# Attention and two MLPs on one core: the first MLP product is taken as (softmax)(state w_in), and part of its squares goes to GpSimd

## Chip, cores and metric

One core of a Trainium2 chip runs the whole program in one launch. The metric is the device time of one execution in microseconds (us), median of several runs; less is better.

## What is computed

```
scores = 0.125 * x @ state^T ; a = softmax(scores) ; xread = a @ state        # per (b, h)
scores2 = 0.125 * state @ x^T ; a2 = softmax(scores2) ; sread = a2 @ x
X = concat([xread, sread]) -> tokens x (h d)                                   # 2176 x 512
h = X @ w_in ; g = where(h >= 1, h, where(h <= -1, 0, (h + 1)^2 / 4)) ; Y = g @ w_out    # 512 -> 2048 -> 512
out = ((Y @ w_a) * (Y @ w_b)) @ w_out2                                         # 512 -> 1536 -> 512
```

There are 4 batches b of 8 heads h, 512 tokens and 32 state rows for each, head width d = 64. Activations come as float32, the weights as 8-byte floats that are turned into float32 on the chip. The tolerance asks for nearly float32 products.

## The kernel before, in words

**Order.** The program records every operation with its engine, its inputs and outputs as byte ranges and PSUM banks, and a rough cost (class `Flow`). `Flow.order` then lays out all engines' instructions: the matmul operations keep the order in which they were recorded, except those marked `loose` (the attention ones), and everything else is placed by due time. All DMAs are issued from one queue, SyncE's (SP), in that order. Each engine works its instructions off strictly in order, with semaphores between engines.

**Products.** A float32 operand is split into a high part (`hi_of`, a ScalarE copy to float32r) and a low part (`tt`, a VectorE subtraction); a product is then three matmuls (`three`, hi*hi, hi*lo, lo*hi), recorded by `mms` (L333 of the profile). Weights are converted by `conv` (L357: the load; L377 or L309: two byte casts on VectorE/ScalarE; L383: a shift-and-or on VectorE).

**Stage one (`phase_one`).** For each of 8 pairs k (half a batch, 4 heads) attention computes scores (`a_qk`, L488), the softmax over 32 state rows (`a_soft`, L504 to L522: transpose, maximum, a subtraction on GpSimd, exp on ScalarE, sum, a multiplication on GpSimd, transpose) and xread (`a_read`, L544 or L536), which is split into the x tiles. `s_soft`, `s_tr` (L596) and `s_read` (L610) make sread. Then `h_mm(j, f)` makes 128 columns f of h for a block j of tokens: 5 blocks of 512, 512, 512, 320 and 320 tokens, 16 values of f, contraction 512 in 4 tiles, so 12 matmuls into one of four PSUM banks. Behind each of these 80 units stand `relu` on ScalarE (L658), `square` on ScalarE, a min/max on VectorE that reads the bank again (L665), and the store of g to DRAM (L300). In this stage the weights w_out (for stage two) are converted too, and part of the second MLP's weights are converted and stored to DRAM as `u_d`.

**Stages two and three.** `v_all` makes the seven operands of a Strassen-like scheme out of w_out, and `b_chunk` runs g @ w_out in three chunks of tokens, each from g loaded back from DRAM, 7 products of 48 matmuls (128 x 368) per chunk. Then `ab_run` and `o_run` do the second MLP. These are L333 matmuls as well.

Of the kernel before, what the change touches and what calls it, by code (L numbers as in the profile page):

```python
# [9 lines left out]
F32 = mybir.dt.float32  # L10
# [9 lines left out]
class Flow:  # L20
# [141 lines left out]
def attention_then_two_mlps(  # L162
# [13 lines left out]
    nc = tc.nc  # L176
# [16 lines left out]
    UA = 4  # L193
    ONDVE = 0
    HALVES = 2
    STEPS = (0, 2, 8, 12, 17, 21, 25, 29)
# [31 lines left out]
    class V2:  # L228
# [97 lines left out]
    def mms(b, cols, pairs, first, last, n, rd, onto=False, off=0):  # L326
# [10 lines left out]
        op({"PE": n * t_mm(cols)}, emit, rd, [bank(b)])  # L337
# [59 lines left out]
    arenas["R0"] = pc.tile([P, R0 // 4], F32R, name="r0")  # L397
# [5 lines left out]
    u_d = pd.tile([F2 + 4, P, 512], F32, name="u_d")  # L403
# [4 lines left out]
    w32_a = Ring([V("F1", 4096 * i, 1024) for i in range(2)])  # L408
# [4 lines left out]
    win = {f: [V("R0", 512 + 8192 * (f // 2) + 2048 * (f % 2) + 4096 * h, 512) for h in range(2)] for f in range(F1)}  # L413
    XAT = [512 + 65536, 512 + 81920, 512 + 114688, 512 + 65536, 512 + 98304]
    x = [[V("R0", XAT[j] + 4 * 4 * BLK[j] * i, 4 * BLK[j]) for i in range(2)] for j in range(NB)]

    def w_in(f, k):
        d, r = conv(w1_k[0, f : f + k], k, stage_a(), z_a(), by="DVE")
        hi, lo = (V("R0", win[f][h].at, 512 * k) for h in range(2))
        hi_of(hi, lambda: d(F32), 512 * k, r, regs(hi))  # L420
        tt(lo, lambda: d(F32), lambda: hi(F32), ALU.subtract, 512 * k, r + regs(hi), regs(lo))

    def aset(arena, o):
        names = (("xld", 1024), ("xn", 1024), ("st", 256), ("t1", 512), ("at", 512), ("a2t", 512))
# [23 lines left out]
    def x_parts(t0, n):  # L448
        done = 0
        while done < n:  # L450
            j = max(i for i in range(NB) if OFF[i] <= t0 + done)
            m = min(n - done, OFF[j] + BLK[j] - t0 - done)
            yield j, t0 + done - OFF[j], done, m
            done += m
# [8 lines left out]
    def a_qk(k):  # L463
# [3 lines left out]
        if "w3" in d:  # L467
            split(*d["s3"], d["st"].sub(128, 128))
        if "x3" in d:
            for i in range(2):  # L470
                split(*(v.sub(512 * i, 512) for v in d["x3"]), d["xld"].sub(512 * i, 512))
            split(*d["q3"], d["st"].sub(0, 128))

            def emit3(e):
                for k, (w, x) in enumerate(three(d["q3"], d["x3"])):
                    for p in range(2):
                        r = slice(64 * p, 64 * p + 64)
                        nc.tensor.matmul(
                            banks[b][r, :], w()[:, r], x()[:, p * 512 : (p + 1) * 512], start=k == 0, stop=k == 2
                        )  # L480

            op({"PE": 0.72}, emit3, regs(*d["q3"], *d["x3"]), [bank(b)], loose=True)
            return
# [8 lines left out]
        op({"PE": 1.8}, emit, regs(d["st"], d["xld"]), [bank(b)], loose=True)  # L492
# [7 lines left out]
    def a_soft(k):  # L500
# [6 lines left out]
            {"DVE": 0.69} if k < ONDVE else {"POOL": 1.35},  # L507
# [793 lines left out]
```

## Time and profile before

| | |
|---|---|
| three runs | 796.75, 798.03, 798.40 us; median 798.03 |
| profiled execution, first to last instruction | 793.9 us |
| TensorE matmul busy | 779.2 us (98%) |
| VectorE busy | 565.4 us (71%) |
| ScalarE busy | 462.5 us (58%) |
| GpSimd busy | 18.8 us (2%) |
| moved by DMA | 130.05 MB, 164 GB/s over the span |

The profiled execution has no run time of its own in the record: its span is 793.9 us, 4.1 us under the median of the runs, which also hold what lies before the first and behind the last instruction. Busy shares are means over stages with different limits, so the prediction reads the first stage by itself.

### The profile page before, as it was taken

The numbers are of one execution on the slowest core, as the hardware profiler recorded it, in microseconds if no ns is written. First come the engines' busy times: TensorE is split into PE (matmuls) and PEld (weight loads), VectorE is DVE, ScalarE is ACT, GpSimd is POOL, SyncE is SP. The second block draws the span as 40 slices with busy tenths as digits, with TensorE's granted clock in tenths as the row PEclk, the third lists the DMA queues.
The fourth block names the chain that finished last, engine by engine and source line by source line (L and its number), as shares of the span: only waits on it lengthen the run. The fifth ranks groups of instructions, "written<-read, shape, count | busy, mean of one in ns | idle before, by whom it ended". The sixth has DMA issues, their size and how long they took to land.

```text
span 793.9 us, 12498 instructions
## 1 busy us (share of the span) xinstructions
PE 779.2 (98%) x4814; PEld 736.8 (93%) x4814; DVE 565.4 (71%) x810; ACT 462.5 (58%) x714; POOL 18.8 (2%) x22
## 2 busy tenths in 40 slices
PE   5999999999999999999999999999999999999998
PEld 3676788879999999999999999999999999999997
DVE  6899863645377885886999897656463679987661
ACT  3889995877676444445665676655422455544440
POOL 2101210000000000000000000000000000000000
PEclk7999999999999999999999999999999999999999
DMA  6879783787226581270433466746151137554211
GB/s 245 295 238 318 246 272 107 247 282 261 91 93 190 165 264 39 79 215 28 130 132 111 131 216 218 242 133 207 55 195 49 37 111 261 170 169 128 99 42 40
DMA packets 76859, 130.05 MB, mean 164 GB/s; under 512 B 6016, under 2 KB 52608, under 8 KB 76800
## 3 DMA queue, kind: packets, MB, share of 16 engines
q1 hardware_dynamic: 76800, 129.26, 49.7%
q8 instruction: 37, 0.61, 0.3%
q14 instruction: 22, 0.18, 0.1%
HBM read 84.93 MB, written 44.30 MB: 163 GB/s over the span
## 4 chain that ended last, share of the span: by engine, by line
PE 87%; DMA 4%; DVE 4%; ACT 3%; issue 1%; SPq 0%; POOL 0%; ACTq 0%; DVEq 0%; POOLq 0%
PE bank L333 84%; DMA f<-in_w_dram 4%; ACT f L309 2%; DVE f L383 1%; PE bank L610 1%; DVE r L318 1%; ACT r L309 1%; DMA f<-in_st_dram 1%; PE bank L488 1%; PE bank L536 0%; DVE f L665 0%; PE bank L596 0%; SPq L297 0%; DVE f L505 0%; DVE f L377 0%
## 5 line engine op out<-in xcount | busy, mean ns | idle before, releaser
L333 PE MATMUL bank<-r 128*128 128x368 f32 (+4 forms) x3048 | 527.7, 330 | 2.7 <-DVE r L318 0.8
L333 PEld LDWEIGHTS bank<-r 128*128 128x128 f32 x3048 | 484.9, 189 | 33.7 <-issue 5.4
L318 DVE TENSOR_TENSOR r<-f,r 128x736 fp32r<-128x736 f32 (+7 forms) x225 | 221.4, 993 | 65.8 <-ACT r L309 62.1
L309 ACT ACTIVATE r<-f 128x736 fp32r<-128x736 f32 (+7 forms) x225 | 193.8, 871 | 123.1 <-PE bank L333 99.4
L333 PE MATMUL bank<-r,r 128*128 128x368 f32 (+2 forms) x1512 | 238.9, 313 | 0.7 <-DVE f L318 0.7
L333 PEld LDWEIGHTS bank<-r,r 128*128 128x128 f32 x1512 | 229.1, 189 | 1.0 <-DVE f L318 1.0
L309 ACT ACTIVATE f<-bank 128x368 f32<-128x368 f32 (+3 forms) x191 | 87.3, 460 | 145.3 <-PE bank L333 144.9
L309 ACT ACTIVATE f<-f 128x512 f32<-128x512 f32 (+5 forms) x157 | 131.5, 854 | 22.3 <-POOL f L508 8.9
L318 DVE TENSOR_TENSOR f<-bank,f 128x368 f32<-128x368 f32 (+2 forms) x168 | 85.3, 517 | 77.0 <-PE bank L333 68.4
L318 DVE TENSOR_TENSOR f<-f 128x256 f32<-128x256 f32 (+6 forms) x146 | 120.0, 843 | 2.1 <-DMA f<-p_d 1.0
L665 DVE SCALAR_TENSOR_TENSOR f<-f,bank 128x512 f32<-128x512 f32 (+1 forms) x80 | 47.4, 602 | 41.2 <-ACT f L309 35.2
L658 ACT ACTIVATE f<-bank,half 128x512 f32<-128x512 f32 (+1 forms) x80 | 49.4, 617 | 29.3 <-PE bank L333 25.2
L383 DVE SCALAR_TENSOR_TENSOR f<-f 128x1024 uint32<-128x1024 uint32 (+1 forms) x39 | 43.7, 1120 | 18.7 <-ACT f L309 18.6
L318 DVE TENSOR_TENSOR f<-f,f 128x736 f32<-128x736 f32 (+1 forms) x24 | 21.6, 909 | 1.0 <-DMA f<-g_d 0.9
L318 DVE TENSOR_TENSOR r<-bank,r 64x64 fp32r<-64x64 f32 (+3 forms) x36 | 14.5, 418 | 7.6 <-ACT r L309 7.4
L610 PEld LDWEIGHTS bank<-f 128*128 128x128 f32 x128 | 15.3, 192 | 1.4 <-ACT f L309 0.9
L610 PE MATMUL bank<-f 128*128 128x64 f32 x128 | 15.3, 273 | 0.1
L309 ACT ACTIVATE r<-bank 64x64 fp32r<-64x64 f32 (+3 forms) x36 | 12.8, 376 | 4.2 <-PE bank L544 1.7
L544 PE MATMUL bank<-f 64*128 64x512 f32 x16 | 5.5, 766 | 5.0 <-DVE f L522 4.9
L488 PE MATMUL bank<-f 128*64 128x512 f32 x32 | 8.6, 617 | 1.2 <-DMA f<-in_st_dram 1.2
L504 DVE STREAM_TRANSPOSE f<-bank 128x512 f32<-128x512 f32 x8 | 5.7, 711 | 5.0 <-PE bank L488 4.9
L544 PEld LDWEIGHTS bank<-f 64*128 64x128 f32 x16 | 1.4, 216 | 7.0 <-DVE f L522 6.3
(33 smaller groups left out, 94.8 us busy)
## 6 DMA issues: line engine op xcount, KB each, us to landing
f<-in_w_dram SPq DMA_DIRECT2D x29, 1024.0 KB, 6.0
f<-p_d SPq DMA_DIRECT2D x17, 768.0 KB, 4.9
g_d<-f SPq DMA_DIRECT2D x48, 256.0 KB, 5.3
f<-g_d SPq DMA_DIRECT2D x32, 368.0 KB, 4.0
p_d<-f SPq DMA_DIRECT2D x48, 184.0 KB, 2.0
f<-g_d SPq DMA_DIRECT2D x16, 352.0 KB, 3.7
f<-in_w_dram SPq DMA_DIRECT2D x10, 512.0 KB, 4.0
g_d<-f SPq DMA_DIRECT2D x32, 160.0 KB, 1.8
```

The costliest lines, as they stand in the source:

```text
L309: lambda e: nc.scalar.activation(dst(), src(), func, **{k: (v() if callable(v) else v) for k, v in kws.items()}),
L318: op({"DVE": t_tt(n)}, lambda e: nc.vector.tensor_tensor(dst(), a(), b(), alu), rd, wr)
L333: nc.tensor.matmul(o, w, x, start=first and k == 0, stop=last and k == n - 1, skip_group_check=onto)
L383: lambda e: nc.vector.scalar_tensor_tensor(out(U32), words_of(1, U32)(), 5, z(U32), ALU.logical_shift_right, ALU.bitwise_or),
L488: nc.tensor.matmul(banks[b][r, :], d["st"]()[:, r], d["xld"]()[:, p * 512 : (p + 1) * 512], start=True, stop=True)
L504: op({"DVE": 0.72}, lambda e: nc.vector.transpose(t1(), banks[b]), [bank(b)], regs(t1))
L544: nc.tensor.matmul(banks[ab], d["st"]()[r, 128:], d["at"]()[r, :], start=True, stop=True)
L610: nc.tensor.matmul(banks[ab][:, p * 64 : (p + 1) * 64], d["xn"]()[:, c * 256 + p * 128 : c * 256 + (p + 1) * 128], d["a2t"]()[:, c * 128 + ...
L658: lambda e: nc.scalar.activation(q(), h(), AF.Relu, bias=half[:, 0:1], scale=0.5),
L665: lambda e: nc.vector.scalar_tensor_tensor(g(), q(), 1.0, h(), ALU.min, ALU.max),
```

## The change

In stage one, xread is no longer formed. For each batch the 256 state rows (8 heads of 32) are multiplied with w_in first: `w_state(b, q, n)` makes, in plain float32 matmuls, 128 of these rows against 512 columns, and splits the result. `h_mm` then takes the softmax weights themselves (8 heads x 32 = 256) as contraction: 2 tiles instead of 4, so 6 matmuls per unit. There are now 4 blocks of 512 tokens; the 128 sread tokens go through `h_state`, plain float32 matmuls without a split. w_in itself is no longer split, nor are x tiles.

```diff
-    def h_mm(j, f, cs=range(4)):
+    def w_state(b, q, n):
+        d = qs[2 * b + q]
+        ab = abank()
+        def emit(e):
+            for p in range(2):
+                r = slice(64 * p, 64 * p + 64)
+                c = (2 * q + p) * P
+                w = win()[:, 2048 * n : 2048 * (n + 1)].rearrange("p (f x) -> p f x", x=512)[:, :, c : c + P]
+                nc.tensor.matmul(
+                    banks[ab][r, :].rearrange("p (f x) -> p f x", x=P), d["st"]()[:, r], w, start=True, stop=True
+                )
+        op({"PE": 1.05}, emit, regs(d["st"], win.sub(2048 * n, 2048)), [bank(ab)])
+        hi, lo = wsum[n][q]
...
+    def h_mm(j, f, cs=range(2)):
...
+            for q in cs:
+                out += three([v()[:, P * o : P * o + P] for v in wsum[n][q]], [v() for v in att[2 * j + q]])
...
+        def square(e):
+            if e == "ACT":
+                nc.scalar.activation(g(), g(), AF.Square)
+            else:
+                nc.gpsimd.tensor_tensor(g(), g(), g(), ALU.mult)
+        op({"ACT": t_act(512), "POOL": 1.1}, square, regs(g), regs(g))
...
+    def h_state(n):
...
+            for i in range(4):
+                w = win.sub(2048 * n + 512 * i, 512)()
+                for c in range(4):
+                    nc.tensor.matmul(
+                        banks[b][:, P * i : P * i + P],
+                        w[:, P * c : P * c + P],
+                        xs()[:, P * c : P * c + P],
...
-    UA = 4
+    UA = 0
+    SWITCH = 48
+    FETCH = (-14, -9, -4, -1)
...
+        if self.gate is not None and size:
+            deps.add(self.gate)
```

The square of each unit is placed by `Flow.order` on ScalarE or on GpSimd (46 of 68 land on GpSimd, L622 of the changed kernel). The memory plan is new: an arena `FS` holds w_in, the attention tiles and four of the seven output buffers, and is given up after unit 48 for `RH` and `F1`, which take the operands of stage two. `flow.gate` keeps some loads (those of w_out, and of the first chunk's g) from being issued before a given unit. The operands of w_out are split in three steps (`v_early`, `v_upper`, `v_rest`). `UA = 0` and the new `w_sums` move eight half-megabyte weight conversions of the second MLP out of stage one: four into the third chunk of stage two, four into stage three.

Names in the rows below: bank_67 to bank_70 are the four banks of h, bank_71 and bank_72 the scores, bank_73 and bank_74 serve `a_read`, `w_state`, `s_tr` and `s_read`; r_65, f_66 and f_89 are the arenas R0, F0 and F1, fs is FS.

TensorE in the middle of stage one. Before, L333 is a unit, L536 a split `a_read`, L488 `a_qk`, L596 `s_tr`, L610 `s_read`:

```order
L333 MATMUL bank_67<-r_65 128x512 x12
L333 MATMUL bank_68<-r_65 128x512 x12
L596 MATMUL bank_73<-ident,f_89 128x128 x4
L333 MATMUL bank_69<-r_65 128x512 x12
L610 MATMUL bank_74<-f_66 128x64 x8
L333 MATMUL bank_70<-r_65 128x512 x12
L488 MATMUL bank_72<-f_66 64x512 x2
```

and now, where L345 is a unit, L524 `w_state`, L575 `s_tr`, L478 `a_qk`, L589 `s_read`:

```order
L345 MATMUL bank_69<-r_65 128x512 x6
L478 MATMUL bank_71<-fs 64x512 x2
L589 MATMUL bank_74<-fs 128x64 x8
L478 MATMUL bank_72<-fs 64x512 x2
L345 MATMUL bank_70<-r_65 128x512 x6
L524 MATMUL bank_73<-fs 64x512 x2
L524 MATMUL bank_74<-fs 64x512 x2
L345 MATMUL bank_67<-r_65 128x512 x6
```

A unit has half the matmuls, the `a_read` rows are gone, and pairs of `w_state` stand in between, 32 of them in all.

GpSimd in stage one. Before, only the softmax steps L508 and L518 stand there, 16 in all:

```order
L508 TENSOR_TENSOR f_89<-f_89 128x512
L518 TENSOR_TENSOR f_89<-f_89 128x512
L508 TENSOR_TENSOR f_66<-f_66,f_89 128x512
L508 TENSOR_TENSOR f_89<-f_89 128x512
L518 TENSOR_TENSOR f_66<-f_66,f_89 128x512
```

and now, where L498 and L508 are the softmax steps and L622 is a square:

```order
L498 TENSOR_TENSOR fs<-fs 128x512
L622 TENSOR_TENSOR f_66<-f_66 128x512 x2
L508 TENSOR_TENSOR fs<-fs 128x512
L622 TENSOR_TENSOR fs<-fs 128x512 x4
L622 TENSOR_TENSOR f_66<-f_66 128x512
L508 TENSOR_TENSOR fs<-fs 128x512
```

Instead of 16 operations GpSimd gets 62, most of them between ScalarE's relu and VectorE's min/max of a unit.

SP's queue at the start. Before, L357 loads w_in, and x, state and x again come from L297:

```order
L297 DMA f_89<-in_xt_dram 128x512 x2
L297 DMA f_89<-in_st_dram 128x256
L297 DMA f_66<-in_xt_dram 128x512 x2
L297 DMA f_66<-in_st_dram 128x256
L357 DMA f_66<-in_w_dram 128x4096 x2
```

and now, where L369 loads w_in, L456 the state and L309 x:

```order
L369 DMA f_66<-in_w_dram 128x4096 x2
L309 DMA fs<-in_xt_dram 128x512 x2
L456 DMA fs<-in_st_dram 128x2x256
L309 DMA fs<-in_xt_dram 128x512 x2
L309 DMA fs<-in_xn_dram 128x1024
L456 DMA fs<-in_st_dram 128x2x256
L309 DMA fs<-in_xn_dram 128x1024
L369 DMA f_66<-in_w_dram 128x2x4096 x2
```

The weights come first, and the two loads of four columns' worth follow behind the first pairs' x and state.

## Rows read from the trace of the kernel before

**Rows 1.** The page, part 1: busy time of each engine, its share, instructions.
```profile
PE 779.2 (98%) x4814; PEld 736.8 (93%) x4814; DVE 565.4 (71%) x810; ACT 462.5 (58%) x714; POOL 18.8 (2%) x22
```

**Rows 2.** Stretches: length, busy time of PE, PEld, DVE, ACT, POOL, clock, DMA, GB/s.
```profile
60.00:80.00 20.00, 19.95 (x93) 13.46 (x93) 18.61 (x35) 18.50 (x32) 3.15 (x3) 1.00 0.92 318
0.00:68.00 68.00, 58.57 (x258) 41.48 (x258) 55.30 (x89) 45.70 (x71) 9.44 (x14) 0.92 0.77 267
241.00:793.90 552.90, 548.05 (x3608) 546.37 (x3606) 407.75 (x546) 280.76 (x417) 0.00 (x0) 1.00 0.43 138
0.00:241.00 241.00, 231.18 (x1209) 190.45 (x1210) 157.60 (x264) 181.76 (x298) 18.78 (x22) 0.98 0.66 223
```

**Rows 3.** Waits of PE, 0 to 250 us: total us, times, longest; the longest one.
```profile
PE bank L544 <- DVE f L522: 4.9, 1, 4.9
```

**Rows 4.** Timeline of PE: start, us, operation, records; some of stage one.
```profile
18.16 4.38 PE L333 MATMUL bank<-r 128*128 128x512 f32 x11 [0.80 <-DVE r L318]
...
59.82 1.13 PE L544 MATMUL bank<-f 64*128 64x512 f32 x4
60.88 1.08 PE L488 MATMUL bank<-f 128*64 128x512 f32 x4
61.89 3.02 PE L333 MATMUL bank<-r 128*128 128x512 f32 x12
...
80.82 0.97 PE L536 MATMUL bank<-r 64*128 64x512 f32 x6
81.72 5.74 PE L333 MATMUL bank<-r 128*128 128x512 f32 x24
...
90.50 1.89 PE L610 MATMUL bank<-f 128*128 128x64 f32 x16
92.20 3.01 PE L333 MATMUL bank<-r 128*128 128x512 f32 x12
...
125.86 5.73 PE L333 MATMUL bank<-r 128*128 128x512 f32 x24
131.44 0.60 PE L596 MATMUL bank<-ident,f 128*128 128x128 f32 x4
131.79 3.00 PE L333 MATMUL bank<-r 128*128 128x512 f32 x12
```

**Rows 5.** Timeline of ACT at the end of stage one.
```profile
238.56 0.53 ACT L658 ACTIVATE f<-bank,half 128x320 f32<-128x320 f32 x1 [0.73 <-PE bank L333]
...
240.32 0.53 ACT L658 ACTIVATE f<-bank,half 128x320 f32<-128x320 f32 x1 [0.73 <-PE bank L333]
...
242.07 2.83 ACT L309 ACTIVATE r<-f 128x1024 fp32r<-128x1024 f32 x3 [0.73 <-PE bank L333]
```

**Rows 6.** Timeline of DVE where instructions stand back to back.
```profile
49.96 0.75 DVE L377 COPY f<-f 128x1024 uint8<-128x1024 uint8 x1 [1.04 <-DMA f<-in_w_dram]
50.61 1.21 DVE L318 TENSOR_TENSOR r<-f,r 128x1024 fp32r<-128x1024 f32 x1
51.74 0.68 DVE L665 SCALAR_TENSOR_TENSOR f<-f,bank 128x512 f32<-128x512 f32 x1
52.40 1.23 DVE L383 SCALAR_TENSOR_TENSOR f<-f 128x1024 uint32<-128x1024 uint32 x1
53.54 0.68 DVE L665 SCALAR_TENSOR_TENSOR f<-f,bank 128x512 f32<-128x512 f32 x1
54.14 0.17 DVE L514 TENSOR_SCALAR f<-f 128x16 f32<-128x16 f32 x1
```

**Rows 7.** Timeline of POOL: one operation by itself, one that lasted twice as long.
```profile
54.74 1.05 POOL L518 TENSOR_TENSOR f<-f,f 128x512 f32<-128x512 f32 x1 [14.49 <-DVE f L515]
...
83.83 2.03 POOL L518 TENSOR_TENSOR f<-f,f 128x512 f32<-128x512 f32 x1
```

**Rows 8.** Timeline of DVE at the same two times.
```profile
54.84 2.04 DVE L318 TENSOR_TENSOR r<-f,r 128x1024 fp32r<-128x1024 f32 x1 [0.24 <-ACT r L309]
...
83.49 1.46 DVE L383 SCALAR_TENSOR_TENSOR f<-f 128x1024 uint32<-128x1024 uint32 x1 [0.66 <-ACT f L309]
```

**Rows 9.** Waits of SP's queue, 0 to 260 us: loads of weights, total, times, longest.
```profile
SPq L357 <- DVE f L383: 20.2, 7, 5.0
SPq L357 <- DVE r L318: 18.2, 10, 5.8
```

More of the change, by code (lines that the diff above doesn't have):

```diff
@@ L417, in w_in @@
+    xs = V("FS", 72704, 4 * P)
     def w_in(f, k):
[L418 to L424, printed above, removed]
+        conv(w1_k[0, f : f + k], k, stage_a(), z_a(), win.sub(512 * f, 512 * k), by="DVE")
@@ L445, in attention_then_two_mlps, with st_load @@
+        return d
+    sets = [aset(i) for i in range(2)]
+    qs = [
+        {**sets[k % 2], "st": V("FS", 32768 + 1024 * (k % 4), 256), "sm": V("FS", 69632 + 256 * (k % 4), 64)}
+        for k in range(NQ)
+    ]
+    qring = Ring(
+        [V("F0", 20608 + 2048 * i, 512) for i in range(3)] + [V("FS", 74752 + 2048 * i, 512) for i in range(4)]
+    )
+    qlast = Ring([V("F0", 2048 * i, 512) for i in range(6)])
     sbank = [4 + k % 2 for k in range(NQ)]
     abank = Ring([6, 7])
[L448 to L454, printed above, removed]
+    def st_load(b):
+        v = V("FS", 32768 + 2048 * (b % 2), 512)
+        op(
+            {"SP": 0.06},
+            lambda e: nc.sync.dma_start(
+                out=v().rearrange("p (k n) -> p k n", k=2), in_=st_d[2 * b : 2 * b + 2].rearrange("k p n -> p k n")
+            ),
+            (),
+            regs(v),
+            1 << 18,
+        )
@@ L465, in a_qk @@
         b = sbank[k]
[L467 to L483, printed above, removed]
         def emit(e):
@@ new lines, in gate @@
+    def gate(b, g, put):
+        h = lambda: banks[b]
+        op(
+            {"ACT": t_act(512) + 0.05},
+            lambda e: nc.scalar.activation(g(), h(), AF.Relu, bias=half[:, 0:1], scale=0.5),
+            [bank(b)],
+            regs(g),
+        )
+        def square(e):
[4 more added lines that the diff above has]
+        op({"ACT": t_act(512), "POOL": 1.1}, square, regs(g), regs(g))
+        op(
+            {"DVE": t_tt(512)},
+            lambda e: nc.vector.scalar_tensor_tensor(g(), g(), 1.0, h(), ALU.min, ALU.max),
+            [bank(b)] + regs(g),
+            regs(g),
+        )
+        put()
@@ L655, in h_mm @@
-        h = lambda: banks[b][:, :n]
-        op(
-            {"ACT": t_act(n) + 0.09},
-            lambda e: nc.scalar.activation(q(), h(), AF.Relu, bias=half[:, 0:1], scale=0.5),
-            [bank(b)],
-            regs(q),
-        )
-        act(q, q, n, AF.Square, regs(q), regs(q))
-        op(
-            {"DVE": t_tt(n)},
-            lambda e: nc.vector.scalar_tensor_tensor(g(), q(), 1.0, h(), ALU.min, ALU.max),
-            [bank(b)] + regs(q),
-            regs(g),
-        )
-        store(lambda: g_d[f, :, OFF[j] : OFF[j] + n], g, [dram("G", f, OFF[j], OFF[j] + n)], 512 * n)
+        g = (qring if 16 * j + f < SWITCH else qlast)()
@@ L761, in b_chunk @@
         n, t0, t1 = CH[c]
-        where = [RAW[(4 * c + i) % 5] for i in range(4)]
+        where = [RAW[(4 * c + i) % 5] for i in ((0, 1, 2, 3) if c else (1, 0, 2, 3))]
         quads = {}
@@ L1119, in phase_one, with a_part, w_part @@
         zero(z_a())
+        def a_part(k):
+            a_qk(k)
+            a_soft(k)
+        def w_part(b, i):
+            w_state(b, i % 2, i // 2)
         a_load(0)
+        st_load(0)
         a_load(1)
```

259 lines of the change are left out of this document (128 added, 131 removed).

## The prediction
> **What bounds the kernel now.** I read the page's busy times first: TensorE (PE) is busy 98% of the span, VectorE (DVE) 71%, ScalarE (ACT) 58%, GpSimd (POOL) 2% [rows 1]. A busy share doesn't say that the matmuls are needed at that pace, so I then asked who PE waited for in the first 250 us: one wait of 4.9 us on the first softmax, and next to nothing behind it [rows 3]. From 18.16 us on, where the units of `h_mm` begin in earnest [rows 4], stage one is bound by PE's own work. It ends at 242.1 us: the last units' relus follow each other at 1.76 us, each ended by PE, and what comes next on ACT waited for PE until 242.07 [rows 5]. Behind it PE is busy 548 of 552.9 us, DVE 408 and ACT 281 [rows 2]. So the time is stage one (242.1) plus a rest that is PE's, and the change acts on stage one.
>
> **PE's work in stage one, before.** In the timeline a unit's price is the distance between starts, since the ends are modelled. Two units of 24 matmuls of 512 columns took 131.44 - 125.86 = 5.58 us, 0.2325 us for each; `a_qk` 61.89 - 60.88 = 1.01 us, a plain `a_read` 1.06, a split one 0.90, `s_read` 1.70, `s_tr` 0.35 [rows 4]. So 48 units of 12 x 0.2325 make 133.9 us, 32 units of 320 tokens at 1.76 [rows 5] 56.3, and attention 8 x 1.01 + 4 x 1.06 + 4 x 0.90 + 8 x 0.35 + 8 x 1.70 = 32.3: 222.5 us. About 3.3 us of this (two `a_qk`, one `a_read`, one matmul) stand ahead of 18.16, so 219.2 should fill 18.16 to 242.1, which is 223.9: the sum is 2% short, and I carry these 2% over.
>
> **PE's work, after.**
> - Units: 64 of 6 matmuls, 384 x 0.2325 = 89.3 us.
> - `w_state`: 32 pairs of float32 matmuls with the shape of `a_qk`, 64 x 512 each: 32 x 1.01 = 32.3 us. Its source is strided; if that cost as much as the other float32 pair, 1.06, it would be 33.9.
> - `h_state`: 64 float32 matmuls of 128 columns. `s_read`'s have 64 columns, 1.70 / 8 = 0.2125 us each; `a_qk`'s 512 columns at 1.01 for two give 0.126 for 128 columns; a price that doubles with the columns would be 0.425. So 8 to 27 us; I take 0.2125, 13.6 us, because it is the row of the nearest size.
> - Attention: 8 x (1.01 + 0.35 + 1.70) = 24.5; `a_read` goes.
>
> The sum is 159.7 us, 62.8 less than before.
>
> **When it can begin.** A unit now needs `w_state`, and that needs four columns of w_in. By the order, 4.5 MiB (4.7 MB) stand on SP's queue up to the load that completes them; at the 267 GB/s of the first 68 us [rows 2] this is 17.7 us. Behind it come a byte cast (0.65 by distance of starts on DVE), a second one on ACT, which I price like DVE's long instructions at 1.13, the shift-and-or 1.14, the matmul pair 1.01 and the two halves of the split at 0.60 each [rows 6]: 5.1 us. With about 1 us of semaphores and issue the first unit starts at 24 us, against 18.16. Two `a_qk` and two `w_state` (4.0 us) can run ahead of that. So PE alone would end stage one at 24 + 1.02 x (159.7 - 4.0) = **182.8 us**.
>
> **DVE is now as near.** Up to the last unit's min/max the order gives DVE 68 min/max, 32 + 8 low halves of 512, 16 transposes, 24 reductions, 11 byte casts or short conversions (159 instructions of the 0.60 class), 35 of 1024 elements (15 conversions, 12 low halves, 8 sums), and some 60 others, 49 of them tiny and 11 of the first chunk. By distance of starts, 0.60 and 1.13 to 1.14 [rows 6], this is 95.4 + 39.6, and I add 15 for the others (none can be under 0.06, the whole at 0.60 would be 36): 150 us. DVE begins when the first weights land, near 6 us. In its densest 20 us before, it was busy 18.61, 93%, with PE unharmed [rows 2]; so it needs at least 6 + 150 / 0.93 = 167 us. ACT has 164 of the short class and 37 of the long one, at those prices 140 us, and is not ahead of DVE. The 46 squares that went to POOL are what brings ACT there.
>
> **What POOL's squares cost DVE.** A POOL operation of 512 elements takes 1.05 us by itself [rows 7]. While one ran at 54.74, a DVE subtraction of 1024 elements took 2.04 us instead of 1.21 [rows 8, 6], and ended 1.1 us behind it: it had not moved until POOL was done. The other way round, POOL's operation at 83.83 took 2.03 [rows 7], with DVE's shift-and-or at 83.49, itself late by 0.23, ahead of it [rows 8]. The Trainium skill, "SBUF — State Buffer", section "SBUF: two separate sides", says the same as a rule: a DVE instruction with two SBUF inputs and a GpSimd one that reads SBUF take a shared pair of ports whole, whoever starts first, and the other blocks. These rows agree with it. The rule speaks against the change: were there no such lock, the squares on POOL would cost DVE nothing. From rows, two-input work on DVE is about 55 us of 180 (18 conversions, 19 low halves, 9 sums, 9 of the first chunk); POOL's 62 x 1.05 = 65 us cover 36% of the stretch. Some 55 instructions then meet it 20 times, at half of 1.05 each: 10 us; the longest delay shown, 0.83, would make it 17. I take 15, and DVE needs 6 + 165 / 0.93 = **183 us**, as much as PE.
>
> **DMA.** Stage one moves 16 MiB of weights, 9 of x and state, 17 of g: 44.0 MB, 232 GB/s over 190 us. Before, it was 223 GB/s as a mean over 241 us and 318 in the densest 20 [rows 2], so it fits, with little left.
>
> **The sum.** Two engines at 183 us that wait for each other in order will not both keep their pace. Between no loss (183) and DVE's whole 7% of slack plus as much again on PE (some 25 us, 208) I take 7 us, nearer to the first, because in 60 to 80 us DVE at 93% cost PE nothing [rows 2]. Stage one ends at 190 instead of 242.1: 52 us less. The rest loses nothing by this sum: eight conversions of half a megabyte are added there, 8 x 0.60 on DVE, which idles 145 of 553 us, and PE's work covers them; uncovered they would be 0 to 5 us. Against the span this is 793.9 - 52 = 742; the median of the runs stands 4.1 us over the span, so the forecast is 798.0 - 52 = **746 us**.
>
> **Rivals.**
> - *No loss at all.* PE keeps 183, or 179 if the loads come at 318 GB/s [rows 2]: 739, at best 735. For it speaks that PE had no waits before. Chance 0.12.
> - *The gate becomes the bound.* A unit's bank is free again after relu, square and min/max, and there are four banks. Back to back, units take 1.4 us, so the three steps must be done within 4 x 1.4 - 1.4 = 4.2 us. Bare they take 0.60 + 1.05 + 0.60; one long DVE job ahead and one lock bring them over 4. The last 16 units stand back to back with the operands of w_out on the same DVE: by the order 20 min/max, 10 long instructions and 11 of the first chunk. If every batch loses 3 to 5 us to it, stage one ends at 197 to 210: 753 to 766. Chance 0.20.
> - *Late conversions show.* The eight conversions in the later stages delay a load of u_d or a product by up to 5 us: 747 to 751. Chance 0.05. It stands for "part of the gain is only moved".
> - *Slower: SP's queue.* All loads and stores stand in one queue. The loads of weights waited 38.4 us there for a stage buffer in 17 waits [rows 9], longest 5.8, at no cost, because a unit took 2.8 us and the stores behind them were not urgent. Now a store that waits behind such a load holds one of seven output buffers, then relu, then a bank, then PE. If all 38.4 us surfaced, the time would be 784. It becomes slower than before only if the 17 loads cost over 3.1 us each (52 us). Against it: the loads of w_out are held back until a given unit, and nine of the 17 loads carry w_in, which PE needs at once anyway. Chance 0.03.
>
> **How the numbers follow.** The main case, stage one ending at 183 to 197, has 0.59 and gives 739 to 753; the forecast is 746. With the rivals of 0.12, 0.20 and 0.05 the range reaches from 735 to 766; what it leaves out is the slower case, and the gate's loss together with `h_state` at its upper bound (14 us more) or with DVE's whole slack, for which I keep a tenth, so that it holds about 0.85. A measurement of this kernel can tell about 0.2% from no change, 1.6 us. Faster: 0.59 + 0.12 + 0.20 + 0.05 = 0.96; the same 0.01; slower 0.03.
>
> **What would show it.** In the profile after: first full unit near 24 us, first 368-column products near 190; `h_mm` matmuls 0.23 us apart, `w_state` pairs 1.0, `h_state` 3.4 us for 16; POOL busy about 65 us and more for blocked ones; DVE over 85% and ACT near 75% in stage one; the stretch behind it as long as 793.9 - 242.1 = 552 us. PE waiting for the min/max (L627) in the last 16 units would speak for the gate, for loads of g or weights for SP. It is wrong if the stretch behind stage one grows by more than 5 us, or if PE waits over 25 us in stage one.

## The result, and the profile after

The change made the kernel faster: 752.19 us (median of four runs, 750.69 to 753.63) against 797.93 for the kernel before beside it, a ratio of 0.9429 with a 95% interval of 0.9406 to 0.9451. That is 45.7 us less, where the forecast had 52; the time lies 6.2 us over the forecast of 746 and inside the range.

The profiled execution of the new kernel took 753.63 us, with a span of 751.9. The other three runs also stand 1.8 us over their spans (750.69 over 748.9, 751.48 over 749.7, 752.9 over 751.1). The runs of the kernel before that were made beside the experiments stand as close to theirs (795.66 over 793.9, 796.67 over 794.9). So of the 4.1 us that the prediction put between the span of before and the median, some 2 were only that this execution was a quick one. The execution profiled now is the slowest of the four, 1.4 us over their median.

First the page of the kernel after, part 1, beside [rows 1]:

```profile
PE 721.4 (96%) x4454; PEld 663.6 (88%) x4454; DVE 562.6 (75%) x790; ACT 433.2 (58%) x656; POOL 76.4 (10%) x67
```

TensorE (PE) has 57.8 us less to do, and the span fell by 42.0. The stretches of the kernel after, with the columns of [rows 2]:

```profile
0.00:24.00 24.00, 9.98 (x36) 5.81 (x38) 14.56 (x26) 7.24 (x11) 4.89 (x10) 0.67 0.81 292
24.00:150.00 126.00, 119.23 (x577) 77.03 (x574) 103.60 (x172) 107.11 (x173) 50.20 (x43) 1.00 0.71 245
150.00:200.00 50.00, 45.90 (x255) 36.97 (x254) 34.69 (x41) 33.45 (x48) 21.27 (x15) 0.97 0.61 206
200.00:751.90 551.90, 546.25 (x3592) 543.80 (x3590) 409.72 (x553) 285.41 (x426) 0.00 (x0) 1.00 0.45 144
...
0.00:198.34 198.34, 173.45 (x854) 118.16 (x855) 151.18 (x236) 146.47 (x228) 76.36 (x67) 0.95 0.69 240
```

From 24 us to the end of stage one PE is busy 94% of the time, less than before; behind stage one it is as full as before (546 of 552 us). VectorE (DVE) is busy 151.2 of stage one's 198.3 us, 76%, ScalarE (ACT) 146.5, 74%. What PE waited for in the kernel after between 26.2 and 198.3 us (total us, times, longest), where before had one wait of 4.9 [rows 3]. L627 is the min/max, L395 the shift-and-or that ends the conversion of a weight, L321 any copy or cast on ACT, L330 any sum or low half on DVE, L613 the relu, L620 a square on ACT, and L622 one on GpSimd (POOL):

```profile
PE bank L345 <- DVE f L627: 4.0, 3, 3.4
PE bank L524 <- DVE fs L395: 3.0, 3, 1.8
PE bank L524 <- ACT fs L321: 2.3, 2, 1.6
PE bank L589 <- ACT fs L321: 0.8, 1, 0.8
PE bank L478 <- DMA fs<-in_st_dram: 0.7, 1, 0.7
```

Together 10.8 us. Where they lie is seen in PE's timeline of the kernel after (columns as in [rows 4]); L345 is now a unit, L524 `w_state`, L658 `h_state`, and the 368-column products are stage two:

```profile
21.94 3.46 PE L524 MATMUL bank<-fs 128*64 128x512 f32 x8 [9.28 <-DVE fs L395]
...
26.18 3.06 PE L345 MATMUL bank<-r 128*128 128x512 f32 x12
...
99.81 5.75 PE L345 MATMUL bank<-r 128*128 128x512 f32 x24
105.49 1.94 PE L524 MATMUL bank<-fs 128*64 128x512 f32 x8
107.35 1.68 PE L345 MATMUL bank<-r 128*128 128x512 f32 x6
...
154.57 14.56 PE L658 MATMUL bank<-fs 128*128 128x128 f32 x128
168.89 15.11 PE L345 MATMUL bank<-r 128*128 128x512 f32 x60
187.43 1.75 PE L345 MATMUL bank<-r 128*128 128x512 f32 x6 [3.43 <-DVE f L627]
189.41 7.09 PE L345 MATMUL bank<-r 128*128 128x512 f32 x24 [0.23 <-DVE f L627]
196.85 1.66 PE L345 MATMUL bank<-r 128*128 128x512 f32 x6 [0.35 <-DVE f L627]
198.34 8.21 PE L345 MATMUL bank<-rh,r 128*128 128x368 f32 x48
```

Read as distances between starts: the first unit at 26.18; a matmul of a unit (105.49 - 99.81) / 24 = 0.237 us; two pairs of `w_state` 107.35 - 105.49 = 1.86; `h_state` 168.89 - 154.57 = 14.3; the last 16 units 198.34 - 168.89 = 29.5, although their 96 matmuls are 22.3 us of work at the 0.2325 of before.

Not all of these 29.5 us is waiting. Behind the wait of 3.43 us TensorE's granted clock fell from 1.00 to 0.50, its lower level of 1.2 GHz; a stretch of the kernel after (columns as in [rows 2]), and below it the same 24 matmuls in a second profiled execution of this kernel (the repetition below), where a wait of 3.44 us left the clock at 1.00:

```profile
189.40:192.00 2.60, 2.59 (x6) 2.11 (x7) 2.55 (x4) 2.04 (x3) 0.00 (x0) 0.50 0.79 296
```

```profile
187.13 5.72 PE L345 MATMUL bank<-r 128*128 128x512 f32 x24 [0.32 <-DVE f L627]
```

They took 7.09 us here and 5.72 there, so some 1.4 us of the 29.5 are the clock's.

Stage one ends at 198.34 instead of 242.1, 43.8 us earlier, and the rest is 751.9 - 198.3 = 553.6 us, against 551.8: it gave 1.8 back.

### The profile page after: what moved, and what is told of

It is laid out like the page before. It is cut to its first block, busy times and chain, and to the rows that moved or that the text cites. A ratio compares the mean times of both kernels' runs of the same rounds, so it can differ in the third digit from the quotient of the medians.

```text
span 751.9 us, 11651 instructions
## 1 busy us (share of the span) xinstructions
PE 721.4 (96%) x4454; PEld 663.6 (88%) x4454; DVE 562.6 (75%) x790; ACT 433.2 (58%) x656; POOL 76.4 (10%) x67
## 4 chain that ended last, share of the span: by engine, by line
PE 81%; DMA 6%; DVE 6%; ACT 2%; POOL 2%; issue 2%; SPq 0%; DVEq 0%; ACTq 0%; POOLq 0%
PE bank L345 74%; DMA f<-in_w_dram 3%; PE bank L524 2%; PE bank L658 2%; ACT f L321 2%; POOL f L622 1%; DMA fs<-in_st_dram 1%; PE bank L478 1%; DVE r L330 1%; DMA p_d<-f 1%; DVE f L627 1%; PE bank L589 1%; DMA f<-p_d 1%; DVE rh L330 1%; DVE fs L395 1%
## 5 line engine op out<-in xcount | busy, mean ns | idle before, releaser
L345 PE MATMUL bank<-rh,r 128*128 128x352 f32 (+2 forms) x1398 | 222.2, 316 | 2.1 <-DVE f L330 0.9
L345 PEld LDWEIGHTS bank<-rh,r 128*128 128x128 f32 x1398 | 215.7, 189 | 3.0 <-DVE f L330 1.2
L321 ACT ACTIVATE f<-bank 128x368 f32<-128x368 f32 (+3 forms) x183 | 82.8, 455 | 142.1 <-PE bank L345 141.7
L345 PE MATMUL bank<-r,r 128*128 128x368 f32 (+1 forms) x960 | 157.5, 316 | 0.0
L345 PEld LDWEIGHTS bank<-r,r 128*128 128x128 f32 x960 | 148.7, 189 | 0.5 <-DVE r L330 0.5
L321 ACT ACTIVATE rh<-f 128x736 fp32r<-128x736 f32 (+5 forms) x120 | 100.7, 845 | 78.9 <-PE bank L345 69.5
L330 DVE TENSOR_TENSOR rh<-f,rh 128x736 fp32r<-128x736 f32 (+5 forms) x120 | 116.1, 972 | 36.3 <-ACT rh L321 33.6
L330 DVE TENSOR_TENSOR f<-bank,f 128x368 f32<-128x368 f32 (+2 forms) x168 | 85.4, 516 | 76.1 <-PE bank L345 65.9
L345 PE MATMUL bank<-r 128*128 128x512 f32 (+1 forms) x582 | 123.1, 363 | 4.1 <-DVE f L627 4.0
L345 PEld LDWEIGHTS bank<-r 128*128 128x128 f32 x582 | 95.0, 191 | 34.0 <-DVE f L627 7.9
L330 DVE TENSOR_TENSOR f<-f 128x256 f32<-128x256 f32 (+7 forms) x142 | 116.8, 842 | 2.9 <-DMA f<-p_d 2.4
L330 DVE TENSOR_TENSOR r<-f,r 128x768 fp32r<-128x768 f32 (+5 forms) x88 | 94.3, 1079 | 18.1 <-ACT r L321 17.7
L321 ACT ACTIVATE r<-f 128x768 fp32r<-128x768 f32 (+5 forms) x88 | 80.7, 924 | 32.2 <-PE bank L345 22.9
L321 ACT ACTIVATE f<-f 128x1024 fp8e5<-128x1024 f32 (+1 forms) x77 | 85.6, 1111 | 17.7 <-DVE f L395 6.3
L345 PE MATMUL bank<-rh 128*128 128x352 f32 (+2 forms) x564 | 93.1, 318 | 0.0
L345 PEld LDWEIGHTS bank<-rh 128*128 128x128 f32 x564 | 88.4, 189 | 0.6 <-DVE f L330 0.6
L345 PE MATMUL bank<-r,rh 128*128 128x368 f32 (+1 forms) x480 | 81.0, 316 | 0.0
L345 PEld LDWEIGHTS bank<-r,rh 128*128 128x128 f32 x480 | 74.7, 189 | 0.2 <-DVE rh L330 0.2
L524 PE MATMUL bank<-fs 128*64 128x512 f32 x128 | 33.1, 632 | 14.5 <-DVE fs L395 12.2
L622 POOL TENSOR_TENSOR f<-f 128x512 f32<-128x512 f32 x25 | 34.1, 1376 | 61.6 <-ACT f L613 61.5
L395 DVE SCALAR_TENSOR_TENSOR f<-f 128x1024 uint32<-128x1024 uint32 (+1 forms) x34 | 33.1, 973 | 6.0 <-ACT f L321 5.9
L627 DVE SCALAR_TENSOR_TENSOR f<-f,bank 128x512 f32<-128x512 f32 x40 | 26.8, 678 | 13.0 <-ACT f L620 6.7
```

The source lines that it names most:

```text
L321: lambda e: nc.scalar.activation(dst(), src(), func, **{k: (v() if callable(v) else v) for k, v in kws.items()}),
L330: op({"DVE": t_tt(n)}, lambda e: nc.vector.tensor_tensor(dst(), a(), b(), alu), rd, wr)
L345: nc.tensor.matmul(o, w, x, start=first and k == 0, stop=last and k == n - 1, skip_group_check=onto)
L395: lambda e: nc.vector.scalar_tensor_tensor(out(U32), words_of(1, U32)(), 5, z(U32), ALU.logical_shift_right, ALU.bitwise_or),
L524: nc.tensor.matmul(banks[ab][r, :].rearrange("p (f x) -> p f x", x=P), d["st"]()[:, r], w, start=True, stop=True)
L622: nc.gpsimd.tensor_tensor(g(), g(), g(), ALU.mult)
```

## The experiments

The question was where the time over PE's own work went (stage one ended at 198.3, PE alone would have ended it at 182.8), and whether the squares on GpSimd (POOL), the four banks or DVE's load had cost it. All ratios are to the kernel before, run on the same chip; all edits but that of "The squares' part alone" are to the kernel after. Each edit is laid out anew by `Flow.order`, so other work of DVE and ACT can move along with it. By the profiles 45 squares stand on POOL in the kernel after, where 46 were given ahead of the prediction.

**All squares on ScalarE.** The rest of the change stays.

```diff
-        op({"ACT": t_act(512), "POOL": 1.1}, square, regs(g), regs(g))
+        op({"ACT": t_act(512)}, square, regs(g), regs(g))
```

> All 68 squares on ScalarE, none on GpSimd; the changed kernel is at 752.2. Theory (GpSimd's squares relieve ScalarE, and cost VectorE by the shared port): VectorE loses no time to GpSimd, but ScalarE gets 46 x 0.6 = 27 us more and stands at some 167 us of work in the 174 us from first unit to end of stage one; it becomes the bound: stage one ends at 198 to 206 and the time is 752 to 760. Rival (the squares on GpSimd only do harm): 745 to 750. Rival (ScalarE would be far over without GpSimd): 770 or more.

Measured: 749.23 us, 0.9395 (0.9365 to 0.9424). My theory, that ACT would then bind, fell; the rival, that POOL's squares do only harm, held. It was repeated beside the unchanged kernel after on one chip:

> The changed kernel unaltered, beside its variants on one chip. All theories: ratio to the kernel before 0.943, within 0.003; it is the yardstick for the next three.

> All squares on ScalarE, the same kernel as in the first of the earlier runs, now beside the changed kernel. Theory (the squares on GpSimd cost VectorE more through the shared port than they spare ScalarE): 2 to 4 us under the changed kernel. Rival (the difference of the earlier runs, 0.9395 against 0.9429 with overlapping intervals, is chance): within 1 us of it.

Measured: the kernel after 752.48 us, 0.9444 (0.9428 to 0.9459); with all squares on ACT 750.21, 0.9415 (0.9402 to 0.9428). The intervals just touch; with the first pair the sign is the same twice, so I take the squares on POOL for a loss of 2 to 3 us. Part 1 of the page, of the kernel after in this repetition:

```profile
PE 721.0 (96%) x4454; PEld 663.7 (88%) x4454; DVE 563.1 (75%) x790; ACT 433.1 (58%) x656; POOL 75.8 (10%) x67
```

and of the one with all squares on ACT:

```profile
PE 722.5 (97%) x4454; PEld 664.6 (89%) x4454; DVE 557.0 (74%) x790; ACT 453.5 (61%) x701; POOL 19.3 (3%) x22
```

DVE does the same 790 instructions in both: POOL's 45 squares lengthened them by 6.1 us in all (by 4.6 in the first pair, 562.6 against 558.0). ACT was spared 20.4 us, 0.45 for each square, and POOL spent 56.5 on them, 1.26 each. Between 24 and 150 us the second kernel's ACT was busy 112.4 of 126 us, 89%, and PE 123.9 (120.8 in the kernel after beside it). PE waited for ACT there for 1.4 us, against 3.1 in the kernel after: ACT at that share held PE up no more than before.

**No squares on POOL in the last 16 units only** (33 of the 45 stay there).

```diff
-    def gate(b, g, put):
+    def gate(b, g, put, tail=False):
...
-        op({"ACT": t_act(512), "POOL": 1.1}, square, regs(g), regs(g))
+        op({"ACT": t_act(512)} if tail else {"ACT": t_act(512), "POOL": 1.1}, square, regs(g), regs(g))
```

> Only the last 16 units' squares are kept on ScalarE; everything before may use GpSimd as in the changed kernel. Theory (the last 16 units took 29.4 us instead of 22.3 because GpSimd's squares and VectorE's two-input work shut each other out): they take 24 to 25 us, time 747 to 748. Rival (VectorE's own work, 26 us busy there, is the bound with or without GpSimd): 752, within 1. Rival (ScalarE, with 8 us more, is the bound there): 753 to 756.

Measured: 748.87 us, 0.9385 (0.9351 to 0.9419). The last 16 units took 195.84 - 170.42 = 25.4 us instead of 29.5, a little over the 24 to 25 expected; the time is about 1 us over what the theory gave. It is as fast as with all 45 squares moved (749.23 and 750.21, overlapping intervals). So the times put the loss on the 12 squares of the last 16 units, and don't show that the other 33 cost anything, though in the profiled executions stage one was some 4 us longer than with all of them moved (table below).

**The squares' part alone, on the kernel before.**

```diff
-        act(q, q, n, AF.Square, regs(q), regs(q))
...
+        op({"ACT": t_act(n), "POOL": 1.1 * n / 512}, square, regs(q), regs(q))
```

> The kernel before with one part of the change alone: squares of the 80 units may go to GpSimd (35 do). Theory (stage one was bound by TensorE, ScalarE's relief is worth nothing there): 798, within 1.5. Rival (the shared port makes VectorE late even there): 800 to 805. Rival (ScalarE's waits counted after all): 793 to 796.

Measured: 799.03 us, 1.0023 (1.0005 to 1.0041). DVE's busy time rose from 565.4 to 571.2 us with 35 squares moved. The loss of 1.8 us (0.4 to 3.3 by the interval) lies between my theory (no more than 1.5 from no change) and the rival of a late DVE (2 to 7 more), and doesn't separate them; a gain from ACT's relief is ruled out. Where PE binds, that relief was worth nothing.

**Eight banks for the last 16 units**, by themselves and together with all squares on ACT.

```diff
+    hlast = Ring([4, 5, 6, 7, 0, 1, 2, 3, 4, 5, 0, 1, 6, 7, 2, 3])
...
-        b = begun.pop((j, f)) if cs[0] else hbank()
+        b = begun.pop((j, f)) if cs[0] else (hbank if 16 * j + f < SWITCH else hlast)()
```

> The last 16 units go round eight PSUM banks instead of four (the attention's four are free by then); squares stay where they are. Theory (the gate: four banks tie TensorE to relu, square and min/max of the unit four back): TensorE runs through the last 16 units in 23 to 25 us, VectorE's backlog is worked off beside the first chunk, time 746 to 748. Rival (VectorE's throughput is the bound: what TensorE gains it loses again on the operands of the first products): 751 to 753.

Measured: 751.74 us, 0.9428 (0.9399 to 0.9457), the same as the kernel after; my theory of 746 to 748 missed. PE's timeline of this kernel:

```profile
166.14 22.35 PE L345 MATMUL bank<-r 128*128 128x512 f32 x96
191.06 2.18 PE L345 MATMUL bank<-rh,r 128*128 128x368 f32 x6 [2.57 <-issue]
194.62 5.89 PE L345 MATMUL bank<-rh,r 128*128 128x368 f32 x18 [1.38 <-DVE f L628]
```

(Lines behind the edit are one higher here: L628 is the min/max.) The 96 matmuls now run without a gap, but the first products of stage two stand still for 2.57 and 1.38 us. The profile names no releaser for the first of these, and the min/max for the second. The banks had been what stopped PE within the 16 units; behind them the min/max and the operands of w_out, on a DVE that POOL holds up, are as late as before. The rival, DVE's throughput, gave 751 to 753 and held.

> All squares on ScalarE, and the last 16 units on eight banks. Theory (with GpSimd out of the way VectorE has about 24 us of work for the last 16 units against TensorE's 22.3, and the first chunk has room for the rest): 1 to 3 us under the variant with four banks. Rival (as with eight banks before: VectorE and ScalarE owe the same work, and TensorE only waits later): the same within 1 us.

Measured: 746.30 us, 0.9364 (0.9347 to 0.9381): 3.9 us under the version with all squares on ACT on the same chip, 6.2 under the kernel after, and the fastest of all; the theory had 1 to 3 under. Its timeline of PE:

```profile
165.24 22.05 PE L345 MATMUL bank<-r 128*128 128x512 f32 x96
187.13 1.16 PE L345 MATMUL bank<-rh,r 128*128 128x368 f32 x6
189.26 7.32 PE L345 MATMUL bank<-rh,r 128*128 128x368 f32 x42 [0.98 <-DVE f L628]
```

Alone, the squares' move gave 2 to 3 us and the banks next to nothing (0.9428 against 0.9429 and 0.9444); together they gave 6.2. But more than the number of banks differs between the two versions with all squares on ACT. Their last 16 units (columns as in [rows 2]), with four banks and with eight:

```profile
166.30:193.26 26.96, 23.06 (x99) 17.80 (x98) 24.89 (x31) 26.02 (x42) 0.00 (x0) 1.00 0.83 288
```

```profile
165.24:187.10 21.86, 21.86 (x99) 18.10 (x98) 18.25 (x24) 20.94 (x34) 0.00 (x0) 1.00 0.87 298
```

DVE did 24.9 us of work there with four banks and 18.3 with eight: the new order puts more of it beside `h_state` (11.3 us against 8.5) and behind the stage. How much of the gain is the banks' and how much this order's was not separated. ACT, busy 26.0 of 27.0 us and 20.9 of 21.9, is near the limit in this stretch.

**The stage boundaries of all these kernels**, from the profiled executions: start of the first unit, from there to the first 368-column product, and the rest of the span (us).

| kernel | first unit | to the end of stage one | rest | median |
|---|---|---|---|---|
| after | 26.18 | 172.2 | 553.6 | 752.19 |
| after, repeated | 24.11 | 171.0 | 555.0 | 752.48 |
| last 16 units' squares on ACT | 26.04 | 169.8 | 552.5 | 748.87 |
| eight banks | 24.38 | 166.7 | 557.9 | 751.74 |
| all squares on ACT | 25.73 | 164.9 | 555.8 | 749.23 |
| the same, repeated | 27.35 | 165.9 | 555.1 | 750.21 |
| squares on ACT, eight banks | 26.04 | 161.1 | 557.2 | 746.30 |
| PE alone, by the prediction | 24 | 158.8 | | |

In the middle column the kernel after is about 6 us over the versions with all squares on ACT (171.6 as a mean against 165.4), of which the clock's 1.4 in one of its two profiles are a part; these are 4.3 over the one with eight banks as well. Only part of each shows in the time, since the start varies by some 3 us, and a stage one that ends earlier finds the rest up to 4 us longer. Why the all-ACT version began 3 us later than its neighbour in the repetition, its first `w_state` at 22.03 instead of 19.86, is open; in the other pair it began no later.

**More work moved to POOL.** All squares on ACT, and eight of the low halves of w_out's operands may go to POOL instead.

```diff
...
-        tt(rows(lo), src, rows(hi, F32), ALU.subtract, n, regs(src, hi), regs(lo))
+        if i in "15":
+            tt(rows(lo), src, rows(hi, F32), ALU.subtract, n, regs(src, hi), regs(lo))
+        else:
+            op({"DVE": t_tt(n), "POOL": 2.2}, ...)
```

> All squares on ScalarE; the ten late low halves of the operands of w_out (1024 elements, SBUF only) may go to GpSimd, 8 do. VectorE's min/max reads PSUM and one SBUF input, which the port rule leaves alone. Theory (VectorE's work is the bound of the last 16 units, 27 us with squares on ScalarE): VectorE is spared 8 x 1.14 = 9 us there, and the stretch becomes 24 us, time 2 to 3 us under the variant without. Rival (ScalarE, at 92% there, is the bound): the same within 1 us. Rival (GpSimd's 2 us operations delay the operands or block VectorE): 1 to 5 us over it.

Measured: 761.92 us, 0.9569 (0.9548 to 0.9589), 11.7 us worse than with all squares on ACT. My theory (2 to 3 us better) had the sign wrong; the rival of POOL's operations in DVE's way had it right, with 1 to 5 us, and the size was twice its upper end. POOL's timeline of this kernel has

```profile
168.85 3.37 POOL L732 TENSOR_TENSOR rh<-f,rh 128x1024 fp32r<-128x1024 f32 x1 [24.41 <-ACT rh L321]
```

DVE's, at the start of stage two:

```profile
192.82 3.17 DVE L330 TENSOR_TENSOR f<-f,f 128x736 f32<-128x736 f32 x1
...
196.51 5.54 DVE L330 TENSOR_TENSOR f<-f,f 128x736 f32<-128x736 f32 x2
```

and PE's:

```profile
209.51 3.74 PE L345 MATMUL bank<-rh,r 128*128 128x368 f32 x11 [7.41 <-DVE rh L330]
```

A sum of 736 columns that takes 0.92 us elsewhere took 3.17 beside POOL, and PE then waited 7.41 us for an operand. DVE's busy time over the whole execution rose from 557.0 to 562.3 us although it had eight low halves of 1.2 us less to do: by these numbers the lock lengthened its work by some 15 us (an estimate).

**The lock by itself.** 28 multiplications of 368 columns, with a result that nothing uses, are added on POOL beside the second of stage two's three chunks, where POOL has nothing else to do.

```diff
+                if c == 1:
+                    probe = V("F0", 52224, n)
+                    op({"POOL": 0.8}, ... nc.gpsimd.tensor_tensor(probe(), hi(F32)[:, 0, :], hi(F32)[:, 1, :], ALU.mult) ..., regs(hi), regs(probe))
```

> In the second chunk of stage two, where GpSimd is idle in the changed kernel, 28 GpSimd multiplications of two SBUF inputs (128 x 368, about 0.8 us) are added, each released by the same high half as VectorE's low half of 736 elements; their result is not used. Theory (a shared port, taken whole by either): the low halves of this chunk, 0.92 us each without it, take 1.1 to 1.7 us as a mean or GpSimd's operations take 1.3 us and more; VectorE's additions that read PSUM and one SBUF input stay at 0.54. Rival (no such lock, the delays in stage one were waits for data): all VectorE durations as without, GpSimd's at 0.8.

Measured: 762.29 us, 0.9559 (0.95 to 0.9618), some 10 us slower than the kernel after, from two runs that lie 6 us apart. DVE's groups by form in that chunk (line, operation, shapes, count | busy us, mean ns | idle before), of the repeated kernel after:

```profile
L330 DVE TENSOR_TENSOR rh<-f,rh 128x736 fp32r<-128x736 f32 x29 | 26.8, 924 | 15.3 <-ACT rh L321 15.1
L330 DVE TENSOR_TENSOR f<-f,f 128x736 f32<-128x736 f32 x8 | 7.3, 919 | 0.0
L330 DVE TENSOR_TENSOR f<-bank,f 128x368 f32<-128x368 f32 x6 | 3.1, 534 | 1.2 <-PE bank L345 1.2
```

and of the probe:

```profile
L330 DVE TENSOR_TENSOR rh<-f,rh 128x736 fp32r<-128x736 f32 x29 | 32.9, 1134 | 15.0 <-ACT rh L321 15.0
L330 DVE TENSOR_TENSOR f<-f,f 128x736 f32<-128x736 f32 x8 | 10.3, 1292 | 0.0
L330 DVE TENSOR_TENSOR f<-bank,f 128x368 f32<-128x368 f32 x6 | 3.1, 533 | 0.2 <-PE bank L345 0.2
```

Sums of two SBUF inputs go from 919 to 1292 ns as a mean, low halves from 924 to 1134; sums that read a bank stay at 533. Single ones in DVE's timeline of the probe:

```profile
284.13 0.91 DVE L330 TENSOR_TENSOR f<-f,f 128x736 f32<-128x736 f32 x1
285.80 1.69 DVE L330 TENSOR_TENSOR f<-f,f 128x736 f32<-128x736 f32 x1
```

Sums of the same size take from 0.91 up to 1.70; POOL's multiplication takes 0.98 to 1.75 us. They aren't slowed in proportion: one waits for the other whole, as [rows 7, 8] already had it. PE waited 3.5 us for low halves in that chunk. The Trainium skill, "SBUF — State Buffer", section "SBUF: two separate sides", states this lock as a rule for DVE instructions with two SBUF inputs; this run agrees, also in that those that read a bank were left alone.

**PE's work raised.** `w_state`'s pair is issued twice, the second over the first.

```diff
-            for p in range(2):
+            for p in (0, 1, 0, 1):
```

> Each w_state issues its pair of matmuls twice (the second pair overwrites the first with the same values): 32.3 us more of TensorE. Theory (stage one is still mostly TensorE's, with some 12 us of waits behind the first units that the ballast can fill): 772 to 782. Rival (VectorE or the loads set the pace, TensorE has room): 752 to 765. Rival (nothing is hidden): 784 or more.

Measured: 779.71 us, 0.9777 (0.9729 to 0.9826), 27.5 us over the kernel after and inside the theory's 772 to 782. Two `w_state` with their second pairs take 178.32 - 174.74 = 3.58 us by distance of starts instead of 1.86, so 32 added pairs are 27.5 us of PE's work, 25.8 of them behind the first unit. PE's first unit, and its first product of stage two:

```profile
28.15 2.11 PE L345 MATMUL bank<-r 128*128 128x512 f32 x8
...
222.67 2.51 PE L345 MATMUL bank<-rh,r 128*128 128x368 f32 x14
```

From the one to the other it took 194.5 us, 22.3 more than in the kernel after and 23.5 more than in its repetition. So most of the added work lengthens the stage: it is still PE's in the main, with 2 to 4 us of waits that the added matmuls fill (PE's waits fell from 10.8 to 6.8 us).

**The planner told of the lock.** A square on POOL is priced at 1.6 us; 39 land there instead of 45.

```diff
-        op({"ACT": t_act(512), "POOL": 1.1}, square, regs(g), regs(g))
+        op({"ACT": t_act(512), "POOL": 1.6}, square, regs(g), regs(g))
```

> The planner's price of a square on GpSimd is 1.6 instead of 1.1 us, which is what they took in the last 16 units; 39 instead of 46 squares land there. Theory (the loss comes from where GpSimd's squares stand, and a plan nearer to the truth avoids some): 749.5 to 751.5. Rival (seven squares less are too few to see): 752, within 1.

Measured: 750.45 us, 0.9413 (0.9382 to 0.9445). The value is where the theory had it, but its interval overlaps that of the kernel after, so this run separates nothing.

## Why the prediction was right, and where it was off

**The gain is PE's work in stage one.** The prediction took 62.8 us off it; PE's busy time fell by 57.8, and 45.7 arrived. The prices held: a unit's matmul 0.237 (0.2325 taken), `h_state` 14.3 (13.6 taken, from `s_read`), a `w_state` pair 0.93 (1.01 taken). The strided source cost nothing that shows: a pair by itself took 127.94 - 126.93 = 1.01 us, as `a_qk` did before. Making PE's work longer made the stage longer.

**The sum of PE and the loss.** Over the 182.8 us for PE alone, stage one lost 15.5 in this profile: 2.2 at the start (26.18 for 24), 6.2 from the first unit to `h_state` (128.4 us for 1.02 x 119.8), 0.4 in `h_state`, and 6.7 in the last 16 units (29.5 for 1.02 x 22.3), the clock's 1.4 among them. In the repetition it ended at 195.12 and lost 12.3: 0.1, 6.0, 0.4 and 5.8. The step that was off is the term "I take 7 us, nearer to the first, because in 60 to 80 us DVE at 93% cost PE nothing": it was mis-sized by about half, 12 to 13 us behind the start. That row was of units of 2.8 us; the new ones take 1.4, so a delay that hid behind the former need not hide behind the latter. Its other ground, two engines at 183 us, fell too (below), so that 7 came as near as it did is in part luck. The 6.2 us stand beside 6.8 us of waits on single late things: `w_state` on a conversion (L395) and on ACT's copies, `s_read` on a copy, `a_qk` on a load of the state.

**The gate rival was right in part.** Its sign was there as written: PE waits for the min/max (L627) in the last 16 units. Stage one ended at 198.3 in the first profile, in the rival's 197 to 210, but at 195.1 in the second, in the main case's 183 to 197. The times, 752.2 and 752.5, lie at the upper end of the main case's 739 to 753. So the totals don't tell the two apart. The rival's place was narrower than given: the last batch only, 5.8 to 6.7 us once, where 3 to 5 in every batch were given.

What held the bank over that wait of 3.43 us can be read off. The unit's last matmul starts at 178.94 us; ACT, POOL and DVE then do, in the kernel after:

```profile
178.34 2.47 ACT L321 ACTIVATE rh<-f 128x736 fp32r<-128x736 f32 x3
180.72 1.04 ACT L321 ACTIVATE r<-f 128x1024 fp32r<-128x1024 f32 x1
181.67 1.99 ACT L613 ACTIVATE f<-bank,half 128x512 f32<-128x512 f32 x3
...
182.42 5.26 POOL L622 TENSOR_TENSOR f<-f 128x512 f32<-128x512 f32 x3 [1.51 <-ACT f L613]
...
182.21 2.59 DVE L330 TENSOR_TENSOR rh<-f,rh 128x736 fp32r<-128x736 f32 x2
184.72 2.06 DVE L330 TENSOR_TENSOR r<-f,r 128x1024 fp32r<-128x1024 f32 x1
186.70 0.67 DVE L627 SCALAR_TENSOR_TENSOR f<-f,bank 128x512 f32<-128x512 f32 x1
```

The relu came 2.3 us late behind four copies of operands of stage two, the square (the first of the three, 182.42 to 184.02) took 1.60 us instead of 0.63 on ACT, and the min/max stood 2.7 us behind two low halves that POOL had blocked (1.76 and 2.05 us instead of 0.92 and 1.21). From the last matmul's end near 179.3 to the free bank at 187.4 it took some 8 us, where four banks allow 4.2. The rival had the form of this sum, with one foreign job and one lock in it; there were several of each.

**"The 46 squares that went to POOL are what brings ACT there"** is wrong as a benefit. With all squares on ACT the kernel was 2 to 3 us faster and ACT, at 89% between 24 and 150 us, not more in the way than before; on the kernel before the move gained nothing. The lock was priced at 15 us of DVE for all 62 operations on POOL, some 11 of them for the squares by number; the squares were measured at 4.6 to 6.1. The neglected price was latency. POOL's squares between relu and min/max took 1.26 us as a mean and up to 2.02 beside DVE, against 0.63 on ACT. DVE's groups by form in the kernel after, 24 to 198 us, with POOL's below:

```profile
L627 DVE SCALAR_TENSOR_TENSOR f<-f,bank 128x512 f32<-128x512 f32 x38 | 25.5, 678 | 13.0 <-ACT f L620 6.7 <-POOL f L622 6.2
L627 DVE SCALAR_TENSOR_TENSOR fs<-fs,bank 128x512 f32<-128x512 f32 x28 | 19.0, 681 | 9.1 <-POOL fs L622 5.8 <-ACT fs L620 3.2
...
L330 DVE TENSOR_TENSOR r<-f,r 128x1024 fp32r<-128x1024 f32 x6 | 9.3, 1546 | 0.0
...
L622 POOL TENSOR_TENSOR f<-f 128x512 f32<-128x512 f32 x25 | 34.1, 1376 | 61.6 <-ACT f L613 61.5
```

Six of the low halves of 1024 columns took 1.55 us instead of 1.21. DVE stood idle 12.0 us for POOL's squares and 9.9 for ACT's; with all squares on ACT it stood idle 17.7 for those. So its idle time as such is not the price; it is paid where a bank is waited for.

**"DVE is now as near"** was too high: 151 us of work including the lock, 76% of the stage instead of over 85%. DVE was late at places, not full. Beside `h_state` it had 14.3 us and used 5.0: in its order the min/max of `h_state`'s own four units came next, each behind PE and ACT, while the order with all squares on ACT had conversions of weights between them and used 8.5 us there.

**The rest** grew by 1.8 us (0 to 5 given; 3.2 in the repetition). **The reference point**: a span 4.1 us under the median was carried over as if every execution had it. The measured distance is 1.8. By spans the forecast was 742 and the result 751.9, 9.9 us apart: 8.3 in stage one (198.3 for 190) and 1.6 behind it. The medians are only 6.2 apart, because the profiled execution of before was a quick one (by some 2.3 us) and that of after a slow one (by 1.4). The medians are the fairer measure of the miss.

**Slower through SP's queue** did not come: in the queue the loads of weights waited 8.8 us for a buffer that DVE held (38.4 before, [rows 9]), and behind the first unit no wait of PE's in stage one was put down directly to a load of weights or to a store. Traced back, though, the longest wait of `w_state` on a conversion (1.85 us, until 58.55) goes to a load of weights from 46.94 to 54.74 us, so a small part of the 6.2 us may be this.

Not tried: an order in which DVE and ACT use the time beside `h_state` while squares stay on POOL, and an earlier start by moving the first conversions ahead of the softmax on DVE.

## What to carry to other kernels

When the bound engine's work is halved in a pipelined loop, price the chain that frees its buffers at the new pace, and by latency: the steps between a unit's last matmul and its free bank must fit in (banks - 1) units, with the foreign jobs that the order puts in front of each of them. Moving an elementwise step to a slower engine didn't help here, because the engine relieved was not in the way; its busy share of 85 to 89% didn't show that, the waits for it did. And when two causes may hold the same place, removing either alone can show little, so try them together as well.

## What the runs showed of the hardware that I had not expected

- The lock between DVE and POOL lengthened DVE's work by 5 to 6 us over 45 squares of 1.04 us (unblocked) in a loop, some 0.1 us each, but by some 15 us over eight low halves of 2.4 us (unblocked), with the kernel 11.7 us slower. The number of operations on POOL was not what decided here.
- The first matmuls of `w_state` behind PE's 9.28 us of idleness took 1057 ns instead of 592, which made two pairs 3.29 us instead of 1.86. In the kernel after the granted clock from 12 to 24 us was 0.50, the level of 1.2 GHz; in the first version with all squares on ACT it read 1.00, 2.4 GHz, with the same 1057 ns. So these rows don't settle that the clock was the cause.
- Behind PE's wait of 3.43 us in the last 16 units the clock fell to 0.50 and 24 matmuls took 7.09 us; in the repetition, behind 3.44 us, it stayed at 1.00 and they took 5.72. The same wait before it had either outcome.
- A float32 matmul of 128 columns cost 0.22 us (14.3 / 64), hardly more than `s_read`'s 0.2125 for 64 columns.
